# Expert 1's rows transposed by DMA instead of TensorE, and expert 0's second pass run with two weight pairs kept

## The chip, the cores and the metric

The program runs on one core of a Trainium2 chip. Its time is the device time of one execution in microseconds; a few executions are timed and the median is given. One further execution is recorded by the hardware profiler. The engines are TensorE (PE in the rows), its weight loads (PEld), VectorE (DVE), ScalarE (ACT), GpSimd (POOL) and SyncE (SP), which issues most transfers.

## The reference

Three stages, each on the output of the one before: block-causal attention, a mixture of 8 experts of which each token takes 2, and a dense layer pair.

```python
def _attn_ref(q, k, v):                       # q, k, v: 4 x 8 x 576 x 64
    scores = np.matmul(q, k.transpose(0, 1, 3, 2)) / np.sqrt(D)
    scores = np.where(mask, scores, -1e9)     # block of 64 rows sees its own and earlier blocks
    return softmax(scores) @ v                # rows of 8 heads joined: x is 2304 x 512
def _moe_ref(x, w_gate, w_noise, noise, w1, w2):
    noisy = x @ w_gate + np.log1p(np.exp(x @ w_noise)) * noise
    # the two largest of 8 per token, weights by softmax of the two
    out[mask] += weight * (np.maximum(x[mask] @ w1[e], 0) @ w2[e])   # 512 -> 1024 -> 512
def _moe2_ref(x, w_in, w_out):                # 512 -> 2048 -> 512
    h = x @ w_in
    return (h * np.clip(h + 3, 0, 6) / 6) @ w_out
```

## The kernel before

Precision is kept by splitting: each float32 operand becomes a rounded high part and the remainder as a low part, and each product is three matmuls, high by high, high by low, low by high (lines 464 to 466 for the first layer of an expert, 1178 to 1180 for the second). The high part of weights is a cast on ScalarE (line 415, `split_hi`), the low part a subtraction (line 419, `split_lo`), on VectorE here. Weights come in pairs of 128-column blocks, four pairs to an expert; `load_raw` (lines 380 and 382) issues two transfers a pair, on ScalarE's queue in the first ten steps of the expert loop.

Attention runs over 16 pairs of heads. It is ordered by a planner (class `Plan`): operations with durations, dependencies and priorities (a smaller number is more urgent) are put in an order by a list schedule, and the order is what is written out for each engine; on the chip the engines wait on semaphores only. A second planner run, `plan2`, orders what lies between attention and the expert loop: the routing of the last batch (`route`), the ranks of the experts by size (`ranks`), the row numbers of all experts (`slot_rows`), and the first pass of expert 0. Expert 0's tokens are known for three of four batches by then, so its first 256 rows (two tiles of 128) go through all eight 128-column blocks during routing. The priorities are in the table `PR`. As soon as the row numbers are there, three gathers on GpSimd (`load_x`, line 1147) fetch expert 0's other three tiles into buffers of the tag `xn`, of which there are five; each is transposed on TensorE (`x_tr`, line 432: four 128x128 transposes into an accumulation bank), rounded on ScalarE (`x_hi`, line 435) and subtracted on VectorE (`x_lo`, line 440). At the end of `plan2` the weight pair 0 is split again for the second pass.

Then comes the expert loop, written out by hand: steps `g`, one 128-column block of one expert each. Steps 0 to 7 are the second pass of expert 0 (columns 256 to 623 of its rows, tiles 2 to 4); steps 8 to 15 are expert 1 (544 rows in two halves of columns, 0 to 271 and 272 to 543), and so on. A step issues in this order: a split of the weight pair after the present one (`split`), at an expert's first step the gathers of the next expert's five tiles, the first layer (`e_s1`), loads of weights, the second layer of the step before (`e_s2`), and work on the next expert's rows. `s1` takes an accumulation bank of two for its output, with a third one (tag `x`) where `third` is set.

For the rows of the next expert there are two ways. Below `FIRST_TURNED` (2, so for expert 1) `x_tile` in steps 2 to 6 transposes one tile a step on TensorE, as above. From `FIRST_TURNED` on, `e_in` (line 1125) parts the 16-bit halves of the float32 row on ScalarE into a `pl` buffer (three of them) and SyncE issues a transposing DMA back into the `xn` buffer (line 1126); two or more steps later `e_out` joins the halves on ScalarE (line 1133) and rounds and subtracts as above, from the joined copy. The table `TURN_X` gives for each of the eight steps which tiles are joined and which are parted: parted are 0 and 1 in step 1, 2 in step 2, 3 in step 4, 4 in step 5; joined are 0 in step 3, 1 in step 4, 2 in step 5, 3 and 4 in step 6.

After the experts the rows are gathered again by token, weighted, and go through the dense layer pair; its weights arrive as 64-bit floats and are converted during the expert loop from step 8 on.

Of the kernel before, what the change touches and what calls it, by code (L numbers as in the profile page):

```python
# [7 lines left out]
F32 = mybir.dt.float32  # L8
# [17 lines left out]
AHEAD = 2  # L26
# [6 lines left out]
XB = 5  # L33
SLACK = 0.58
PLANES = ("w64", "ca", "w64", "cm")
TURNED = 2
FIRST_TURNED = 2
TURN_X = (((), ()), ((), (0, 1)), ((), (2,)), ((0,), ()), ((1,), (3,)), ((2,), (4,)), ((3, 4), ()), ((), ()))
CONV = (8, 5)
STICK = 2.77  # L40
# [3 lines left out]
PRE = ((0, 0), (1, 0))  # L44
WLS = ({"DVE": 1.2}, {"DVE": 1.14, "POOL": 2.4}, {"POOL": 2.4, "DVE": 1.14}, {"POOL": 2.4})
VHS = ({"POOL": 2.3}, {"DVE": 0.42}, {"POOL": 2.3, "DVE": 0.42}, {"DVE": 0.42, "POOL": 2.3}, {"ACT": 0.65, "DVE": 0.42})
PR = {'last': -400, 'ranks': 30, 'rows': -20.0, 'hold': 0.2, 'na': -563.0, 'nb': 803.0, 'lsel': (0, 0, 1, 0, 0, 0, 0, 0, 0, 0), 'f1': (-44.4, -71.8, 11.1, 5.5, -74.0, -35.6, -184.8, -17.0), 'f2': (-11.9, -48.6, 26.7, -35.2, 51.6, 79.6, -22.3, -2.7), 'fa': (-27.7, 2.3, 6.9, -8.3), 'fb': (-0.5, 4.2, -119.4, 2.2), 'fh': (12.0, -77.5, -123.7, -2.4, -13.0, -59.6, 12.4, 13.5), 'fl': (1.5, 3.1, -75.2, 108.2, -1.2, 70.3, 3.8, 16.9), 'v': -317.22, 'qk': -13.33, 'keep': 1, 'S': -2.19, 'max': -82.24, 'exp': -40.31, 'pt': 0.29, 'hi': 360.75, 'lo': -37.22, 'hid': True, 'av': 7.35, 'o': 252.33, 'od': True, 'inv': 36.95, 'fin': 28.78, 'x': -1.53, 'route': -0.9, 'rp': 1, 'route2': 6.36, 'xt': -802.7, 'eg': 587.2, 'ex': 432.13, 'ew': 2149.25, 'first': 0, 'sel': 2, 'vh': 3, 'wl': 1, 'wa': -418.9, 'wb': 581.9, 'h': -328.4, 's2': -471.5, 'vs': (-0.62, -2.53, 0.92, 0.17, 0.59, -5.66), 'vpt': (28.74, 8.73, -37.77, -2.51, -5.17, 6.9, -0.23, 1.96), 'vp': (-2.81, -6.08), 'vf': (15.46, 3.5)}
CLAMP = 122879.9921875


# [7 lines left out]
class Plan:  # L58
# [11 lines left out]
    def add(self, eng, fn, deps=(), prio=0.0, take=None, drop=None, lat=None, after=0.0, port=False, kind=None):  # L70

        if drop is not None:
            drop.left += 1
        self.ops.append((eng, fn, {d for d in deps if d is not None}, prio, take, drop, lat, port, kind))
        self.ready.append(after)
        return len(self.ops) - 1
# [110 lines left out]
def kernel(  # L187
# [216 lines left out]
    GR = [[(c, 0) for c in (1, 2)], [(c, 0) for c in range(3, NC)] + [(0, b) for b in range(0, B, 2)]]  # L404
    GR += [[(c, b) for c in range(1, NC)] for b in range(1, B)]
    PS = list(range(NPF)) + [st[0] * NPF + st[1] // 2 for st in STEPS[::2]]
    U0 = len(PS)
    PS += [NP + p for _ in GR for p in range(NFF // 2)]
    w_s = {}
# [728 lines left out]
    def turned_tile(key, t, n, to):  # L1138
# [3 lines left out]
        x_hi(to, t, x)  # L1142
        x_lo(to, t, x)

    def load_x(e, t):
        a = work.tile([128, DM], F32, tag="xn", name="xn", bufs=XB)
        nc.gpsimd.indirect_dma_start(
            out=a, out_offset=None, in_=x_tok[:, :],
            in_offset=bass.IndirectOffsetOnAxis(ap=(slot_ids if e else ids)[:, e * NT + t:e * NT + t + 1], axis=0),
        )  # L1150
        xn[e, t] = a
# [13 lines left out]
    def s2(tiles, h, wb, f, first, last, rows=None):  # L1165
        hh, hl = h
        wh, wl = wb
        for t in tiles:
            if first:
                yps[t] = ps_y.tile([128, DM], F32, tag=f"y{t}", name=f"y{t}")  # L1170
            n = min(128, (rows or CAP) - t * 128)
            if rows and t == NT - 1 and n <= 64:
                sl = slice(t * 128, t * 128 + 2 * n)
                nc.tensor.matmul(yps[t][:2 * n], lhsT=hh[:, sl], rhs=wh[:, f % 2], start=first, stop=False)
                nc.tensor.matmul(yps[t][:2 * n], lhsT=hh[:, sl], rhs=wl[:, f % 2], start=False, stop=last)
                continue
            sl = slice(t * 128, t * 128 + n)
            nc.tensor.matmul(yps[t][:n], lhsT=hh[:, sl], rhs=wh[:, f % 2], start=first, stop=False)  # L1178
            nc.tensor.matmul(yps[t][:n], lhsT=hh[:, sl], rhs=wl[:, f % 2], start=False, stop=False)  # L1179
            nc.tensor.matmul(yps[t][:n], lhsT=hl[:, sl], rhs=wh[:, f % 2], start=False, stop=last)  # L1180
# [227 lines left out]
    for f in range(NF + 1):  # L1408
        pr = 10 + 2 * f
        if f < NF and f % 2 == 0:  # L1410
            k2["wa", f // 2] = wops(0, f // 2, [k2.get(("s1", f - 4 + i)) for i in range(2)], pr + PR["wa"] + PR["fa"][f // 2])
        if f < NF and f % 2 == 0:
            k2["wb", f // 2] = wops(1, f // 2, [k2.get(("s2", f - 4 + i)) for i in range(2)], pr + PR["wb"] + PR["fb"][f // 2])
        if PR['first'] <= f < NF:
            g = Bank("h", 1)

            def first(e, f=f, g=g):
                ps = ps_y.tile([128, 512], F32, tag=f"y{NT - 1}", name="h") if g.bank == 2 else None
                g.tile = s1("a", f, f // 2, 0, n_, ps=ps)

            def second(e, f=f, g=g):
                hT["a", f] = h_tiles()
                h_hi(hT["a", f], g.tile, 0, n_)

            k2["s1", f] = add({"PE": 1.31}, first, [k2.get(("wa", f // 2))], pr + PR["f1"][f], take=g)
            hh = add({"ACT": 0.27}, second, [k2["s1", f], k2.get(("s2", f - HB))], pr + PR["h"] + PR["fh"][f], drop=g)
            k2["h", f] = add({"DVE": 0.34}, lambda e, f=f, g=g: h_lo(hT["a", f], g.tile, 0, n_), [hh], pr + PR["h"] + PR["fl"][f], drop=g)
        if f:
            k2["s2", f - 1] = add({"PE": 1.3}, lambda e, f=f - 1: s2(range(AHEAD), hT.pop(("a", f)), w_s[1, f // 2], f,
                                                                     f == 0, f == NF - 1),  # L1430
                                  [k2.get(("h", f - 1)), k2.get(("wb", (f - 1) // 2)), k2.get(("s2", f - 2))], pr + PR["s2"] + PR["f2"][f - 1])
    counts = work.tile([128, 16], F32, tag="counts", name="counts", bufs=1)[:, 0:E]
# [34 lines left out]
    c_ = add({"DVE": 1.75}, lambda e: ranks(psum(gn)), [c_], PR["ranks"], drop=gn, port=True)  # L1467
    add({"DVE": 1.4}, lambda e: slot_rows(), [c_, dp["id"]], PR["rows"], port=True)
    for t in range(AHEAD, NT):
        k2["g", t] = add({"POOL": 1.25}, lambda e, t=t: load_x(0, t), [dp["id"]], -10 + t, lat=3.0)  # L1470
        xops(t, k2["g", t], PR["xt"] + t)
    wops(0, NPF, [k2["s1", NF - 4], k2["s1", NF - 3]], PR["na"])
    wops(1, NPF, [k2["s2", NF - 4], k2["s2", NF - 3]], PR["nb"])
    plan2.run(busy, PR['last'] + 20, PR['hold'])
    gctx.close()
    wraw2[0] = ctx.enter_context(tc.tile_pool(name="wraw2", bufs=4, side="right", reuse_waits="tile"))
# [1 line left out]
    rr = route_rows()  # L1478
    NG = len(STEPS)
    conv = conv_ops()  # L1480
    last_use = {r: u for u, r in enumerate(PS)}
    load_at = {}
    for r in range(NPF, len(raw_q)):
        load_at.setdefault(max(2 * (last_use[r - 8] - NPF) if r >= 8 else 0, r - NPF), []).append(r)
    for g in range(NG + 1):
        u = NPF + g // 2 + 1
        if g < NG:
            e, f, _, _ = STEPS[g]
            if g % 2 == 0:
                split(0, u)  # L1490
            if f == 0 and e + 1 < E:
                for t in range(NT):
                    load_x(e + 1, t)
            if wide and g == CONV[0] - 1:
                conv_load(0)
            if g % 2 == 1:
                split(1, u)
            e_s1(g, FIRST_TURNED <= e + 1 and g < NG - NF)
            for r in load_at.get(g, ()):
                load_raw(r + 1, nc.scalar if g < 10 else None)  # L1500
        if g > NF and g % 3 == 0 and g // 3 - NF // 3 <= OVF // 4:
            zero_rows(g // 3 - NF // 3 - 1)
        if g == NF:
            nc.gpsimd.memset(zero, 0.0)
            for i in range(E):
                n = CAP - CAPS[i]
                nc.sync.dma_start(y_tab[i * CAP + CAPS[i]:(i + 1) * CAP].rearrange("p (k n) -> p k n", k=KD),
                                  zero[0:n, None, :].to_broadcast([n, KD, 128]))
        if wide and g >= CONV[0]:
            for _ in range(CONV[1]):  # L1510
                next(conv, None)
        if g == NG:
            overflow()
        if g:
            e_s2(g - 1)
        if g == NG - NF:
            for t in range(len(GR[0])):
                gather(0, t)
        for _ in range(2):
            if next(rr, None) == 0:  # L1520
                overflow_count()
        if g < NG and f >= 2 and f - 2 < NT and e + 1 < min(E, FIRST_TURNED):
            x_tile(e + 1, xn.pop((e + 1, f - 2)), f - 2, CAP)
        if g < NG and FIRST_TURNED <= e + 1 < E:
            outs, ins = TURN_X[f]
            for t in outs:
                e_out(e + 1, t)
            for t in ins:
                e_in(e + 1, t)
        if NG - NF + 4 <= g < NG - NF + 4 + len(GR[0]):  # L1530
            combine(0, g - (NG - NF + 4))
        if NG - NF + 5 <= g < NG - NF + 5 + len(GR[0]):
            combined(0, g - (NG - NF + 5))
# [93 lines left out]
```

## Time and profile before

| | us |
|---|---|
| median of 3 timed runs | 1066.28 (1065.69 to 1066.46) |
| profiled execution, whole | 1065.57 |
| profiled execution, span | 1063.8 |
| TensorE busy / VectorE / ScalarE / GpSimd, of the span | 1049.2 / 776.3 / 593.8 / 317.3 |

The mean granted TensorE clock is 0.998. The span is the time from the first to the last recorded instruction of the profiled execution. In the rows, a line of a timeline gives the start, the busy time, the engine (a `q` behind its name is its instruction queue), the line, the operation, output and inputs, the count, and in brackets how long the engine was idle before and what ended that. Durations of matmuls are modelled to the end of a pipeline, so that one starts before the one ahead of it has ended.

### The profile page before, as it was taken

Reading aid. Unit: us, or ns where it says so; the run is one execution under the profiler, and the core shown is the slowest. Engines: PE = TensorE matmul, PEld = TensorE weight load, DVE = VectorE, ACT = ScalarE, POOL = GpSimd, SP = SyncE. Lnnn points to the kernel's source line nnn. Section 1 sums busy time; section 2 is a strip of 40 time slices with the busy share of each in tenths; the row PEclk is TensorE's granted clock in tenths of the full one; section 3 lists DMA queues with packets and bytes.
Section 4 is the critical chain, followed back from the end, with each engine's and each line's share of the span. In section 5 each row is a group of like instructions: output and inputs, shape, how many; then the busy total and the mean of one; then the engine's idle time right before and its main releaser. Section 6 shows DMA issues by size and latency. Waiting matters only on the chain. (4 is left out here: it accounts for less than half of the span.)

```text
span 1063.8 us, 16944 instructions
## 1 busy us (share of the span) xinstructions
PE 1049.2 (99%) x6075; PEld 921.5 (87%) x6075; DVE 776.3 (73%) x1470; ACT 593.8 (56%) x1121; POOL 317.3 (30%) x379
## 2 busy tenths in 40 slices
PE   7999999999999999999999999999999999999998
PEld 6999999988988999999888898988888888888886
DVE  8878787878588998988787856775746755664442
ACT  6777777754456555655555445564535444454442
POOL 7558787713101120202020002733501511310000
PEclk9999999999999999999999999999999999999999
DMA  7534532114999999898887525212202211201001
GB/s 193 147 91 130 130 91 58 22 45 138 339 280 334 298 296 298 266 230 246 205 246 206 165 72 197 70 60 60 60 1 70 51 40 50 59 10 40 1 1 40
DMA packets 163573, 141.80 MB, mean 133 GB/s; under 512 B 92373, under 2 KB 131381, under 8 KB 163485
## 3 DMA queue, kind: packets, MB, share of 16 engines
q1 hardware_dynamic: 147501, 102.79, 35.2%
q0 software_dynamic: 8640, 28.32, 8.8%
q10 hardware_dynamic: 7344, 9.57, 2.7%
q8 instruction: 49, 0.80, 0.3%
q14 instruction: 39, 0.32, 0.1%
HBM read 92.94 MB, written 36.70 MB: 122 GB/s over the span
## 5 line engine op out<-in xcount | busy, mean ns | idle before, releaser
L464 PE MATMUL h<-xh,wah 128*128 128x512 f32 (+8 forms) x832 | 272.5, 328 | 0.7 <-ACT xh L435 0.7
L465 PE MATMUL h<-xl,wah 128*128 128x512 f32 (+8 forms) x832 | 271.2, 326 | 0.9 <-DVE xl L440 0.9
L466 PE MATMUL h<-xh,wal 128*128 128x512 f32 (+8 forms) x832 | 271.3, 326 | 0.0
L1179 PE MATMUL y<-wbl,hh 128*128 128x512 f32 (+1 forms) x576 | 225.7, 392 | 0.2
L1178 PE MATMUL y<-wbh,hh 128*128 128x512 f32 (+1 forms) x576 | 225.7, 392 | 0.1
L1180 PE MATMUL y<-wbh,hl 128*128 128x512 f32 (+1 forms) x576 | 225.0, 391 | 0.0
L464 PEld LDWEIGHTS h<-xh,wah 128*128 128x128 f32 x832 | 156.3, 188 | 16.2 <-ACT xh L435 1.1
L465 PEld LDWEIGHTS h<-xl,wah 128*128 128x128 f32 x832 | 156.4, 188 | 15.9 <-DVE xl L440 1.3
L466 PEld LDWEIGHTS h<-xh,wal 128*128 128x128 f32 x832 | 156.3, 188 | 11.5
L1180 PEld LDWEIGHTS y<-wbh,hl 128*128 128x128 f32 (+1 forms) x576 | 107.3, 186 | 24.8
L1179 PEld LDWEIGHTS y<-wbl,hh 128*128 128x128 f32 (+1 forms) x576 | 107.3, 186 | 21.5 <-POOL wbl L419 0.8
L487 ACT ACTIVATE hh<-h 128x288 fp32r<-128x288 f32 (+7 forms) x128 | 53.2, 417 | 130.2 <-PE h L466 129.7
L1178 PEld LDWEIGHTS y<-wbh,hh 128*128 128x128 f32 (+1 forms) x576 | 107.3, 186 | 21.2 <-issue 0.6
L1541 DVE SCALAR_TENSOR_TENSOR r<-r,h 128x512 f32<-128x512 f32 (+1 forms) x80 | 50.5, 631 | 98.2 <-ACT r L1540 98.0
L1540 ACT ACTIVATE r<-h,three 128x512 f32<-128x512 f32 (+1 forms) x80 | 51.6, 645 | 118.7 <-PE h L466 118.7
L419 DVE TENSOR_TENSOR wal<-wa,wah 128x1024 fp32r<-128x1024 f32 x80 | 106.3, 1328 | 11.2 <-ACT wah L415 10.2
L419 DVE TENSOR_TENSOR wbl<-wb,wbh 128x1024 fp32r<-128x1024 f32 x76 | 102.5, 1348 | 15.1 <-ACT wbh L415 14.9
L415 ACT CAST wbh<-wb 128x1024 fp32r<-128x1024 f32 x80 | 83.8, 1048 | 24.8 <-PE y L1180 14.6
L1543 ACT CAST hh<-r 128x512 fp32r<-128x512 f32 (+1 forms) x80 | 46.2, 577 | 86.0 <-DVE r L1541 86.0
L1544 DVE TENSOR_TENSOR hl<-r,hh 128x512 fp32r<-128x512 f32 (+1 forms) x80 | 56.0, 700 | 51.5 <-ACT hh L1543 51.5
L804 ACT ACTIVATE P<-sb,nm 128x192 f32<-128x192 f32 (+4 forms) x144 | 74.7, 528 | 29.1 <-DVE nm L798 29.0
L415 ACT CAST wah<-wa 128x1024 fp32r<-128x1024 f32 x80 | 83.7, 1046 | 2.4 <-DVE rm L1249 1.5
(275 smaller groups left out, 1780.9 us busy)
## 6 DMA issues: line engine op xcount, KB each, us to landing
wa<-in_moe_w_dram SPq DMA_DIRECT2D x23, 512.0 KB, 5.1
wb<-in_moe_w_dram SPq DMA_DIRECT2D x23, 512.0 KB, 5.6
y_tab<-yo SPq DMA_DIRECT2D x32, 256.0 KB, 4.3
w<-in_moe_w_in_dram SPq DMA_DIRECT2D x16, 512.0 KB, 5.3
y_tab<-zero SPq DMA_DIRECT2D x8, 1024.0 KB, 8.5
w<-in_moe_w_out_dram SPq DMA_DIRECT2D x16, 512.0 KB, 5.5
x_tok<-x SPq DMA_DIRECT2D x32, 144.0 KB, 2.8
wa<-in_moe_w_dram ACTq DMA_DIRECT2D x9, 512.0 KB, 6.6
```

The lines of the kernel that those rows point to most:

```text
L415: nc.scalar.copy(w_s[which, u][0], raws[PS[u]][which])
L419: (nc.gpsimd if e == "POOL" else nc.vector).tensor_tensor(lo, raws[PS[u]][which], hi.bitcast(F32), op=OP.subtract)
L464: nc.tensor.matmul(ps, lhsT=wh, rhs=xh, start=first, stop=False)
L465: nc.tensor.matmul(ps, lhsT=wh, rhs=xl, start=False, stop=False)
L466: nc.tensor.matmul(ps, lhsT=wl, rhs=xh, start=False, stop=last)
L487: nc.scalar.activation(h[0][:, c0:c1], ps[:, :c1 - c0], AF.Relu)
L804: nc.scalar.activation(o, views.pop((p, i)), AF.Exp, bias=nms.pop((p, i)), scale=1.0, accum_out=rs[p % 3][:, i:i + 1])
L1178: nc.tensor.matmul(yps[t][:n], lhsT=hh[:, sl], rhs=wh[:, f % 2], start=first, stop=False)
L1179: nc.tensor.matmul(yps[t][:n], lhsT=hh[:, sl], rhs=wl[:, f % 2], start=False, stop=False)
L1180: nc.tensor.matmul(yps[t][:n], lhsT=hl[:, sl], rhs=wh[:, f % 2], start=False, stop=last)
L1540: nc.scalar.activation(r[:, :n], ps[:, :n], AF.Relu, bias=three, scale=1.0)
L1544: nc.vector.tensor_tensor(hl[:, :n], r[:, :n], hh[:, :n].bitcast(F32), op=OP.subtract)
```

## The change

The rows of expert 1 take the second way too (`FIRST_TURNED` is 1): parted, transposed by DMA, joined, during steps 1 to 6; with it the first layer of expert 0's second pass uses the third accumulation bank. The second pass of expert 0 takes the weight pairs in the order 2, 3, 0, 1; pairs 2 and 3 are the last ones split in the first pass, and their splits are used again, so that pair 2 and 3 are not split a second time (`KEPT`); the two splits at the end of `plan2` and the two of steps 0 and 1 are gone. The three `xn` buffers of expert 0's late tiles are taken and touched early by a one-column write on GpSimd (`make_x`). The priorities of `plan2` are others, and the planner's durations for the two layers of the first pass are 1.345 and 1.385 instead of 1.31 and 1.3. By the new order the load of the tenth weight pair moves from step 5 to step 6.

```diff
-FIRST_TURNED = 2
+FIRST_TURNED = 1
-PR = {'last': -400, 'ranks': 30, 'rows': -20.0, 'hold': 0.2, 'na': -563.0, 'nb': 803.0, 'lsel': (0, 0, 1, 0, 0, 0, 0, 0, 0, 0), ... 'xt': -802.7, ... 'wa': -418.9, 'wb': 581.9, 'h': -328.4, 's2': -471.5, ...
+PR = {'last': -1000, 'ranks': 30, 'rows': 20.0, 'hold': 0.1, 'lsel': (0, 0, 0, 0, 0, 0, 0, 0, 0, 0), ... 'xt': -870.4, ... 'wa': -775.6, 'wb': 1670.1, 'h': -862.4, 's2': -314.7, ...
...
     PS = list(range(NPF)) + [st[0] * NPF + st[1] // 2 for st in STEPS[::2]]
+    KEPT = {NPF: NPF - 2, NPF + 1: NPF - 1}
+    PS[NPF:2 * NPF] = list(KEPT.values()) + list(range(NPF - 2))
...
+    def make_x(t):
+        xn[0, t] = work.tile([128, DM], F32, tag="xn", name="xn", bufs=XB)
+        nc.gpsimd.memset(xn[0, t][:, 0:1], 0.0)
+
     def load_x(e, t):
-        a = work.tile([128, DM], F32, tag="xn", name="xn", bufs=XB)
+        a = xn[e, t] if (e, t) in xn else work.tile([128, DM], F32, tag="xn", name="xn", bufs=XB)
...
-            k2["s1", f] = add({"PE": 1.31}, first, [k2.get(("wa", f // 2))], pr + PR["f1"][f], take=g)
+            k2["s1", f] = add({"PE": 1.345}, first, [k2.get(("wa", f // 2))], pr + PR["f1"][f], take=g)
...
     for t in range(AHEAD, NT):
-        k2["g", t] = add({"POOL": 1.25}, lambda e, t=t: load_x(0, t), [dp["id"]], -10 + t, lat=3.0)
+        made = add({"POOL": 0.1}, lambda e, t=t: make_x(t), [], -2000 + t)
+        k2["g", t] = add({"POOL": 1.35}, lambda e, t=t: load_x(0, t), [dp["id"], made], -10 + t, lat=3.2)
         xops(t, k2["g", t], PR["xt"] + t)
-    wops(0, NPF, [k2["s1", NF - 4], k2["s1", NF - 3]], PR["na"])
-    wops(1, NPF, [k2["s2", NF - 4], k2["s2", NF - 3]], PR["nb"])
     plan2.run(busy, PR['last'] + 20, PR['hold'])
...
-    last_use = {r: u for u, r in enumerate(PS)}
+    last_use = {r: u for u, r in enumerate(PS) if u not in KEPT}
+    for which in range(2):
+        for u, v in KEPT.items():
+            w_s[which, u] = w_s[which, v]
...
-            if g % 2 == 0:
+            if g % 2 == 0 and u not in KEPT:
                 split(0, u)
...
-            if g % 2 == 1:
+            if g % 2 == 1 and u not in KEPT:
                 split(1, u)
             e_s1(g, FIRST_TURNED <= e + 1 and g < NG - NF)
```

## Rows read from the trace of the kernel before

**Rows 1.** The page's first part: busy time, share of the span, instructions.
```profile
PE 1049.2 (99%) x6075; PEld 921.5 (87%) x6075; DVE 776.3 (73%) x1470; ACT 593.8 (56%) x1121; POOL 317.3 (30%) x379
```
**Rows 2.** TensorE's waits in the span: us in total, times, longest us.
```profile
...
PE h L465 <- DVE xl L440: 0.9, 2, 0.6
PE h L464 <- ACT xh L435: 0.7, 1, 0.7
PE xps L432 <- DVE idt L1456: 0.5, 1, 0.5
...
```
**Rows 3.** Timeline of TensorE, 251 to 257 us.
```profile
254.66 0.63 PE L432 MATMUL xps<-ident,xn 128*128 128x128 f32 x4 [0.48 <-DVE idt L1456]
...
256.69 0.44 PE L465 MATMUL h<-xl,wah 128*128 128x368 f32 x1 [0.29 <-DVE xl L440]
```
**Rows 4.** Timeline of TensorE, steps 1, 2, 3 and 8 of the expert loop.
```profile
262.71 0.33 PE L464 MATMUL h<-xh,wah 128*128 128x368 f32 x1
...
266.78 0.60 PE L432 MATMUL xps<-ident,xn 128*128 128x128 f32 x4
...
271.28 0.60 PE L432 MATMUL xps<-ident,xn 128*128 128x128 f32 x4
...
289.31 0.29 PE L464 MATMUL h<-xh,wah 128*128 128x272 f32 x1
...
290.83 0.28 PE L464 MATMUL h<-xh,wah 128*128 128x272 f32 x1
```
**Rows 5.** Timelines of VectorE and GpSimd: row numbers, first and third gather.
```profile
246.48 0.20 DVE L637 SCALAR_TENSOR_TENSOR ids<-idacc 128x40 int32<-128x40 f32 x1
...
247.51 1.44 POOL L1147 DMA_INDIRECT xn<-x_tok,ids  x1 [5.40 <-ACT hh L487]
...
251.12 0.95 POOL L1147 DMA_INDIRECT xn<-x_tok,ids  x1 [0.30 <-issue]
```
**Rows 6.** Engines' busy time and VectorE's costliest group, 229 to 256.6 us.
```profile
229.00:256.60 27.60, 25.64 (x174) 22.33 (x174) 25.23 (x90) 14.16 (x24) 5.58 (x5) 1.00 0.19 50
...
L419 DVE TENSOR_TENSOR wal<-wa,wah 128x1024 fp32r<-128x1024 f32 x4 | 4.9, 1218 | 0.5 <-ACT wah L415 0.4
```
**Rows 7.** ScalarE: groups of 305 to 339 us; timeline of step 1.
```profile
L1133 ACT COPY pl<-xn 128x1024 uint16<-128x1024 uint16 x5 | 6.8, 1366 | 2.5 <-DMA xn<-pl 2.5
...
L415 ACT CAST wah<-wa 128x1024 fp32r<-128x1024 f32 x3 | 3.1, 1049 | 0.0
...
L1125 ACT COPY pl<-xn 128x1024 uint16<-128x1024 uint16 x3 | 3.1, 1039 | 0.0
L435 ACT CAST xh<-pl 128x512 fp32r<-128x512 f32 x5 | 3.1, 622 | 0.2
...
264.89 0.48 ACT L487 ACTIVATE hh<-h 128x368 fp32r<-128x368 f32 x1 [0.58 <-PE h L466]
...
265.60 0.38 ACTq L382 DMA_DIRECT2D wb<-in_moe_w_dram  x1
```
**Rows 8.** Transposing DMAs: all 30; one issued in 325.4-327; one in 426-429.
```profile
DMA to landing us min/median/max: 3.1/6.6/9.9
...
xn<-pl SPq DMA_TRANSPOSE x1, 5.0
...
xn<-pl SPq DMA_TRANSPOSE x1, 3.1
```
**Rows 9.** Timelines, expert 1 to 2: last tile parted, joined; TensorE starts.
```profile
324.55 1.04 ACT L1125 COPY pl<-xn 128x1024 uint16<-128x1024 uint16 x1
...
332.51 1.37 ACT L1133 COPY pl<-xn 128x1024 uint16<-128x1024 uint16 x1
...
337.71 0.29 PE L464 MATMUL h<-xh,wah 128*128 128x288 f32 x1
```
**Rows 10.** Timelines of VectorE and TensorE near 7 us: parts of one tile.
```profile
6.50 1.15 DVE L773 SCALAR_TENSOR_TENSOR kl<-raw_k,kh 128x320 fp32r<-128x320 f32 x1
...
6.95 0.28 PE L790 MATMUL sb<-kl,qd0h 128*128 128x256 f32 x1
```

## What the change will do to the time

> **What bounds the kernel now.** I read the page's busy line first: TensorE (PE) is busy 99% of the span [rows 1]. Then all of PE's waits, grouped by what ended them: only three entries concern the experts, 2.1 us together, and all lie between 229 and 257 us [rows 2]; the others belong to attention, which the change leaves as it is. So a change can gain in two ways only: fewer PE instructions, or a shorter wait in that stretch. Then the PE timeline. In the second pass of expert 0 (steps 0 to 7 of the loop) the period is plain: step 1 runs from 262.71 to 266.78, 4.07 us; step 2, which carries four transposes of expert 1's rows, from 266.78 to 271.28, 4.50 us [rows 4]. Five steps carry them.
>
> The wait before the second pass lies at its three late row tiles: PE stands until the transposes of tile 4 at 254.66 (0.48 idle), again for its high part (0.7), again for its low part until 256.69 (one of the two in the 0.9) [rows 2, 3]. Behind tile 4 is the third gather: the row numbers are computed at 246.48, the first gather is issued at 247.51, the third at 251.12 [rows 5], and 3.5 us later PE transposes its rows.
>
> **The change part by part.** The sum is made against the profiled execution (1065.57 us, span 1063.8); the median of the three timed runs is 0.7 above it, and I add that at the end.
>
> *Expert 1's transposes leave PE.* 20 transposes in five steps: 5 x (4.50 - 4.07) = 2.2 us less PE work, all on the path, since PE waits for nothing in those steps [rows 2, 4]. This is certain as far as the rows go.
>
> *ScalarE does more.* Per tile it copies the halves apart (1.04), joins them (1.37) and rounds the result from SBUF (0.62, in place of a like rounding from PSUM) [rows 7]: 5 x 2.4 = 12 us more in eight steps of 4.07 us. Four casts of 1.05 are gone with the kept pairs [rows 7], two of them in these steps. The copies are hidden only as long as the last tile is ready when expert 1 begins. I follow ScalarE from the start of step 0, calling that 0. The activation of step g can start at 4.07 g + 2.2 (step 1: PE starts at 262.71, the activation is at 264.89 [rows 4, 7]). Step 4: activation at 18.5, two weight loads issued behind it until about 19.6 (the second issue starts 0.7 after the activation and is 0.4 long [rows 7]), tile 1 joined and rounded 2.0, tile 3 parted 1.0: 22.6. Step 5: cast 1.0, activation 0.5, tile 2 joined 2.0, tile 4 parted 1.0: 27.1. Then the transposing DMA, L us from issue to landing; then join and round 2.0, and VectorE's low part with its hand-over 0.9: ready at 30.0 + L. The first matmuls of expert 1 cover columns 0 to 271, so tiles 0 to 2; the second half starts 1.52 later [rows 4]. That the first half need not wait for the last tile is shown early in the span: a matmul at 6.95 reads part of a tile whose other part VectorE writes from 6.50 to 7.65 [rows 10]. So tile 4 is wanted at 8 x 4.07 + 1.5 = 34.1, and PE stands for L - 4.0. It stands at least 0.5, because step 6 issues two pairs of loads (four issues, some 2.2 us, from about 27.5) ahead of the joins of tiles 3 and 4 on ScalarE's queue: 29.7 + 4.0 + 0.9 = 34.6.
>
> For experts 2 and later the same chain has room: tile 4 parted at 324.55, joined at 332.51, PE starts the next expert at 337.71 [rows 9], because their steps work on five row tiles; expert 0's second pass has three, and that is the weak place of this change.
>
> L is not in the trace for this stretch. The ends are 3.1 and 9.9 us, the median 6.6; 3.1 belongs to a stretch in which nearly nothing else moved; 5.0 is a pair's first in a loaded stretch [rows 8]. I take 5.0: SP's queue carries nothing else in steps 1 to 6, and in steps 4 and 5 only one pair of weights is loaded, but two pairs come right behind the transpose. Stall 1.0; bounds 0.5 and 5.9.
>
> The rows show a transpose of the same 256 KB at three times its least time once other DMAs run [rows 8]. The Trainium skill, "DMA: Bandwidth & Descriptors", section "Latency and other measured facts", gives a DMA transpose 261 GB/s, and its section "Anatomy of one DMA" a fixed part of 2.0 us; an estimate from the two is 3.0 us, which agrees with the lowest row and would make the stall 0.5 and the time 1063.2. Its section "Issuing engines are not separate DMA queues" (all transfers interleave on the same 16 engines) speaks against counting on that here.
>
> *Kept pairs.* The order 2, 3, 0, 1 removes four casts on ScalarE and four subtractions on VectorE, of 1.22 each [rows 6]. Neither is on PE's path by itself. Two subtractions of them lay in the first pass, where VectorE is busy 25.2 of 27.6 us [rows 6], so demand falls to about 22.8. Loads: pair 1 of the third expert in turn is loaded one step later; it is used some ten steps on, so nothing.
>
> *Planner order, early buffers.* The last batch's routing gets a priority above all else, and the row buffers are touched on GpSimd (POOL) in advance. The first gather starts 0.83 after the row numbers end (246.68 to 247.51); behind the later list, whose buffers were free, it is a few tenths [rows 5], so about 0.55 is saved there. The rest depends on how much earlier the row numbers come. On VectorE's queue splits and low parts stand between the links of the routing chain; putting less than one split (1.22) behind it gives 0.9. Together 1.4. The upper bound is the whole wait: 1.45 of shown idle (0.48, 0.68, 0.29) plus some 0.2 for each, because modelled ends of matmuls overlap the next start: 2.1. The lower bound is below nothing: each split put behind routing comes later for PE in the first pass, up to a split and a low part, 1.6.
>
> *The rest.* The third accumulation bank for this pass costs nothing and removes no wait. The first wait, at the start of the first pass (the other in the 0.9 [rows 2]), comes from attention's end and stays. ScalarE is the engine behind whose loads the joins queue in step 6; SP's queue gets five transposes ahead of the conversion's first load, which then goes out after them, and is not used before step 8.
>
> Sum: 2.2 + 1.4 - 1.0 = 2.6 us less: 1063.0 for a profiled execution, 1063.7 as a median.
>
> **Rivals.**
> 1. Nothing is late: transposes land in 3.1, routing wins all. 2.2 + 2.1 - 0.5 = 3.8: 1062.5. For it: ScalarE's copies may overlap more tightly than I add them. Against: two pairs of loads in step 6.
> 2. The last tile is late by the median row: L = 6.6, stall 2.6, net 1.0: 1065.3. For it: nearly all transposes under load lie at 5 or above [rows 8].
> 3. Routing first starves PE in the first pass: the wait moves from the late tiles to the splits, gain there 0, net 1.2: 1065.1. For it: VectorE has little free time there [rows 6]; against: 2.4 us of its work are gone.
> 4. Slower: the same place as rival 2, with the longest row. From L = 7.6 the stall (3.6) eats all that the rest brings; at 9.9 it is 5.9, net loss 2.3: 1068.6. Against: 9.9 is one of 30, and SP's queue is emptier here.
> That the change doesn't do what it says is excluded for the transposes (they are gone from the code); for the routing it is rival 3.
>
> **How the numbers follow.** Forecast 0.45, rival 1 0.17, rival 2 0.20, rival 3 0.11, rival 4 0.07. What a measurement can tell from no change is about 0.2%, 2.1 us. The forecast's own spread (L of 4.5 to 5.5, routing 0.9 to 1.9) is about 0.8 either way, so 0.32 of its 0.45 lies beyond 2.1, with rival 1 0.49 faster; 0.44 the same; 0.07 slower. The range runs from just beyond rival 1, 1062.2, past rivals 2 and 3 to 1067.0, where L is 8.3.
>
> **What would show it.** Period of steps 2 to 6 of the second pass 4.07 us, no transposes on PE. Second pass starting 1.4 earlier than 256.7, with the row numbers about 0.9 earlier and a first gather a few tenths behind them. A wait of about 1 us on PE about 1.5 us into expert 1, ended by the low part of its last tile, and ScalarE idle there for the transposing DMA. I am wrong if that wait is above 2 us or missing, if PE waits inside the first pass for a split, or if expert 1 waits at its first matmul.

## The result, and the profile after

| | before | after |
|---|---|---|
| median of 5 timed executions, us | 1066.18 (1065.69 to 1066.46) | 1081.66 (1078.63 to 1083.68) |
| profiled execution, whole / span, us | 1065.57 / 1063.8 | 1083.68 / 1081.9 |

The ratio is 1.014, with a 95% interval of 1.0128 to 1.0151: the changed kernel is 15.5 us slower, where 2.6 us less were forecast; the time lies 14.7 us above the upper end of the range. The new one also scatters by 5 us from execution to execution, the old one by 0.8. Between the profiled executions, of which that of the changed kernel is the slowest of its five, the difference is 18.1 us, and that is the one I account for.

TensorE's busy time (first part of the page) is 4.3 us up on [rows 1], though 20 transposes are gone from it:

```profile
PE 1053.5 (97%) x6055; PEld 923.2 (85%) x6055; DVE 771.8 (71%) x1467; ACT 600.3 (55%) x1127; POOL 315.2 (29%) x381
```

What PE waited for, in the view of [rows 2] (us in total, times, longest us); line numbers are two higher than before as far as `e_out`, now line 1135, and six higher from `load_x`, now line 1153, to the second layer:

```profile
PE y L1184 <- ACT hh L489: 8.0, 2, 7.0
PE h L466 <- ACT xh L437: 5.5, 1, 5.5
...
PE h L467 <- DVE xl L442: 0.9, 2, 0.6
PE h L466 <- issue: 0.7, 1, 0.7
...
PE y L1186 <- DVE hl L493: 0.6, 1, 0.6
```

The 0.9 and the 0.7 are those of [rows 2]. The rest is new: 14.2 us. The timeline of PE shows where:

```profile
282.09 0.50 PE L1184 MATMUL y<-wbh,hh 128*128 128x512 f32 x1 [1.04 <-ACT hh L489]
...
283.43 0.50 PE L1186 MATMUL y<-wbh,hl 128*128 128x512 f32 x1 [0.61 <-DVE hl L493]
...
294.38 0.80 PE L1184 MATMUL y<-wbh,hh 128*128 128x512 f32 x1 [6.98 <-ACT hh L489]
...
305.99 0.59 PE L466 MATMUL h<-xh,wah 128*128 128x272 f32 x1 [5.54 <-ACT xh L437]
```

The last line is the second half of step 8, the first matmul that reads the last tile of expert 1. The long wait before it, for the activation `hh` of step 6, is no wait for rows. ScalarE's timeline says what stood ahead of that activation:

```profile
262.19 1.99 ACT L1127 COPY pl<-xn 128x1024 uint16<-128x1024 uint16 x2 [0.72 <-issue]
...
266.73 1.05 ACT L1127 COPY pl<-xn 128x1024 uint16<-128x1024 uint16 x1 [1.21 <-issue]
...
271.92 1.35 ACT L1135 COPY pl<-xn 128x1024 uint16<-128x1024 uint16 x1 [2.52 <-DMA xn<-pl]
...
277.76 1.35 ACT L1135 COPY pl<-xn 128x1024 uint16<-128x1024 uint16 x1 [2.51 <-DMA xn<-pl]
...
281.56 0.47 ACT L489 ACTIVATE hh<-h 128x368 fp32r<-128x368 f32 x1
290.08 1.33 ACT L1135 COPY pl<-xn 128x1024 uint16<-128x1024 uint16 x1 [8.05 <-DMA xn<-pl]
...
291.97 1.04 ACT L1127 COPY pl<-xn 128x1024 uint16<-128x1024 uint16 x1
...
293.86 0.47 ACT L489 ACTIVATE hh<-h 128x368 fp32r<-128x368 f32 x1
...
303.96 1.33 ACT L1135 COPY pl<-xn 128x1024 uint16<-128x1024 uint16 x1 [7.75 <-DMA xn<-pl]
```

Line 1127 parts a tile, line 1135 joins one. Tile 2 is parted by 267.78 and can be joined at 290.08: 22.3 us for the transposing DMA and its issue. ScalarE stands idle for 8.05 us of that, with tile 4's parting (291.97) and the activation of step 6 (293.86) behind the join in its queue. Tile 4 is thus parted only by 293.01, 37.0 us after step 0 began; where no loads ran beside the transposes (an experiment below) it was 25.2 us. Its own DMA then takes 10.95, from 293.01 to 303.96. The first two tiles, parted by 263.2 and 264.2, were joined at 271.92 and 277.76.

Granted clock (columns of the view of [rows 6]; the number after the engines is the clock as a share of full speed, then DMA share, GB/s):

```profile
290.00:292.00 2.00, 0.00 (x0) 0.00 (x0) 0.00 (x0) 1.88 (x3) 0.32 (x1) 0.95 1.13 247
292.00:294.00 2.00, 0.00 (x0) 0.00 (x0) 0.70 (x2) 2.00 (x4) 0.63 (x1) 0.50 0.94 211
294.00:296.00 2.00, 1.50 (x3) 0.78 (x4) 1.97 (x4) 1.97 (x3) 0.17 (x1) 0.50 1.03 372
296.00:298.00 2.00, 2.00 (x5) 1.49 (x6) 0.78 (x2) 0.21 (x1) 0.78 (x1) 0.50 1.05 352
298.00:300.00 2.00, 2.00 (x13) 1.81 (x12) 0.00 (x0) 0.00 (x0) 0.00 (x0) 0.84 1.10 336
...
306.00:308.00 2.00, 1.87 (x6) 1.56 (x7) 1.74 (x2) 2.00 (x3) 0.72 (x2) 0.50 0.69 208
308.00:310.00 2.00, 2.00 (x9) 1.90 (x9) 1.97 (x6) 0.88 (x3) 0.00 (x0) 0.50 0.90 202
310.00:312.00 2.00, 2.00 (x7) 1.49 (x6) 1.93 (x7) 0.01 (x1) 0.00 (x0) 0.50 1.01 342
312.00:314.00 2.00, 2.00 (x14) 1.81 (x13) 1.93 (x4) 0.00 (x0) 0.00 (x0) 0.93 1.12 339
```

While PE stood before 294.38 the clock fell to its lower level, 1.2 GHz, and stayed there for some 4 us of work; the same after the second stand, for some 6. Summed over these stretches, PE's busy time times the share of the clock that was missing is 5.1 us.

The account: step 0 starts at 255.97 (before: 255.96), step 9 at 312.79 (before: 294.36), 18.4 us later. New waits 14.2, half clock 5.1, transposes gone -2.2 (five times 0.43): 17.1. Of the other 1.3 us half is in the modelled ends of matmuls: from the start of one matmul to the start of the next the four stands cost 0.16 more each than their idle time (the last is 5.83, less the 0.13 by which its neighbours follow each other, against 5.54). The rest I did not find in single rows. After step 9 the difference changes by only 0.3, from 18.4 to 18.1.

### The profile page after: what moved, and what is told of

It reads as the page before. It is cut to its first block, busy times and chain, and to the rows that moved or that the text cites. A ratio compares the mean times of both kernels' runs of the same rounds, so it can differ in the third digit from the quotient of the medians.

```text
span 1081.9 us, 16914 instructions
## 1 busy us (share of the span) xinstructions
PE 1053.5 (97%) x6055; PEld 923.2 (85%) x6055; DVE 771.8 (71%) x1467; ACT 600.3 (55%) x1127; POOL 315.2 (29%) x381
## 5 line engine op out<-in xcount | busy, mean ns | idle before, releaser
L1185 PEld LDWEIGHTS y<-wbl,hh 128*128 128x128 f32 (+1 forms) x576 | 108.2, 188 | 20.8
L421 DVE TENSOR_TENSOR wal<-wa,wah 128x1024 fp32r<-128x1024 f32 x78 | 103.8, 1331 | 12.9 <-ACT wah L417 11.5
L421 DVE TENSOR_TENSOR wbl<-wb,wbh 128x1024 fp32r<-128x1024 f32 x74 | 100.0, 1352 | 16.2 <-ACT wbh L417 14.3
L493 DVE SCALAR_TENSOR_TENSOR hl<-h,hh 128x288 fp32r<-128x288 f32 (+8 forms) x128 | 56.2, 446 | 41.4 <-ACT hh L489 37.3
```

What stands on the lines that cost most here:

```text
L421: (nc.gpsimd if e == "POOL" else nc.vector).tensor_tensor(lo, raws[PS[u]][which], hi.bitcast(F32), op=OP.subtract)
L493: nc.vector.scalar_tensor_tensor(h[1][:, c0:m], ps[:, :m - c0], 0.0, h[0][:, c0:m].bitcast(F32), op0=OP.max, op1=OP.subtract)
```

## Experiments

Three theories of why the rows of expert 1 come late. **Theory 1:** the transposing DMAs, alone on SP's queue, get a small share of the engines while the weight loads come from ScalarE's queue. **Theory 2:** the stretch has too many bytes to move, from whichever queue. **Theory 3:** ScalarE's 12 us of copies do not fit, and the DMA's time does not matter. Ratios are to the kernel before on the same chip, with 95% intervals.

**The change without the new way for expert 1.**

```diff
-FIRST_TURNED = 1
+FIRST_TURNED = 2
```

> The changed kernel with FIRST_TURNED back at 2: expert 1's rows are transposed by PE again; the pair order 2, 3, 0, 1, the kept pairs, the early row buffers and the new planner orders stay. All three theories below put the loss on the transposing DMAs and give 1065.5 to 1066.5 us here: the second pass of the changed kernel began at 256.70 us as before, so I now count the kept pairs at nothing, where the prediction counted -1.4. If kept pairs or orders cost something by themselves, it is over 1067.

Measured 1066.93 us, ratio 1.0006 (0.9997 to 1.0015): no difference that can be told. So kept pairs, early buffers and new orders do not make the loss, nor do the orders and buffers bring the 1.4 us forecast for them (the prediction had the 1.4 there, and not at the kept pairs, as the expectation says). From the end of PE's wait at the start of the first pass to step 0 it is 25.8 us here, 26.0 before.

**The new way alone, in the kernel before.**

```diff
-FIRST_TURNED = 2
+FIRST_TURNED = 1
```

> The kernel before with FIRST_TURNED at 1 and nothing else: the transposing DMAs for expert 1 without kept pairs. If the transposing DMAs alone make the loss, about 1078 to 1084 us, with waits of 5 to 7 us of PE for expert 1's rows. If it needs the kept pairs' order too (which moves the loads of steps 4 to 7), under 1070.

Measured 1077.74 us, ratio 1.0127 (1.0099 to 1.0156), 0.3 under the range of the first theory. The new way alone makes nearly the whole loss, by the same two kinds of wait; PE's timeline of this run:

```profile
280.21 0.50 PE L1178 MATMUL y<-wbh,hh 128*128 128x512 f32 x1 [2.58 <-ACT hh L487]
...
297.93 0.47 PE L464 MATMUL h<-xh,wah 128*128 128x272 f32 x1 [2.97 <-ACT xh L435]
```

The waits are shorter than the 5 to 7 us expected, in an execution of 1074.54 us, the fastest of the four; in it the first two transposes were the slow ones, joined 12 and 16 us after their parting, and the last took 7.

**Without the five transposing DMAs.**

```diff
-        nc.sync.dma_start_transpose(...)
+        if e != 1:
+            nc.sync.dma_start_transpose(...)
...
+        how = "p (n w) -> p w n" if e == 1 else "p (w n) -> p w n"
```

> The changed kernel without the five transposing DMAs of expert 1; ScalarE makes the same copies, and expert 1 computes on rows that were not transposed (that part of the output is left wrong). Theories 1 and 2 (the DMA's landing is what is late): 1062 to 1064.5 us, with PE waits for expert 1's rows of under 1 us, which would also be the forecast's rival 1. Theory 3 (ScalarE's 12 us of copies are too much for these steps, or stand in the wrong place): over 1070 us, hh still late.

Measured 1065.12 us, ratio 0.9989 (0.9979 to 0.9998). All of ScalarE's copies are there (the join reads its rows in another order here, in the same 1.36 us), and PE waits for no row of expert 1. Theory 3 falls. Against the run with PE's transposes on the same chip (1066.93) it is 1.8 us less: that is what the transposes are worth on the path, 2.2 forecast. The time is 0.6 above the 1062 to 1064.5 expected; those numbers still held the 1.4 us that the run before last doesn't show.

**Loads on SP's queue.**

```diff
-                load_raw(r + 1, nc.scalar if g < 10 else None)
+                load_raw(r + 1)
```

> The changed kernel with one word changed: the weight loads of the first ten steps are issued by SP, as those of the later steps are, not by ScalarE. Theory 1 (the transposing DMA's packets get a small share while loads come from ScalarE's queue): each transposing DMA lands 4 to 9 us after its issue, PE's waits shrink to under 2 us, 1063 to 1068 us. Theory 2 (too many bytes in these steps, whatever the queue): landings stay at 9 to 21 us, 1078 to 1084 us. Theory 3 (ScalarE's in-order copies hold h_hi up, the DMA's time does not matter): 1078 to 1084 us.

Measured 1070.99 us, ratio 1.0036 (1.0024 to 1.0048): over two thirds of the loss is gone with the same bytes and the same copies, for one word. It is theory 1's direction, though not down to its 1068. From the views of PE's waits and of the transposing DMAs (256 to 292 us):

```profile
PE h L466 <- ACT xh L437: 2.3, 1, 2.3
```

```profile
DMA to landing us min/median/max: 5.6/7.7/9.9
```

In the changed kernel the same view has 12.6/12.8/12.9 for those it could pair, without the one of over 20 us.

**A plain copy of the same bytes in the transpose's place.**

```diff
+        if e == 1:
+            nc.sync.dma_start(src.bitcast(U16), pl)
+        else:
             nc.sync.dma_start_transpose(...)
```

> The changed kernel, its loads from ScalarE's queue as they are, but for expert 1 the transposing DMA is a plain copy of the same 256 KB from the one tile to the other (2,048 bytes of a row at a time, so expert 1's rows are not transposed and that part of the output is left wrong). If the small packets of the transpose (256 bytes each) are what gets a small share beside the loads: landings of 3 to 6 us, waits of PE under 1.5 us, 1064.5 to 1067 us. If any DMA on SP's queue gets half the share or less while ScalarE's queue loads: landings of 8 us and more, 1072 us or more.

Measured 1067.76 us, ratio 1.0014 (1.0005 to 1.0024): 0.8 over the upper end of the one theory and far below the 1072 of the other. Loads on ScalarE's queue beside a plain copy on SP's do little harm. All transfers from 264 to 276 us, first of the changed kernel, then of this run (q1 is SP's queue, q10 ScalarE's, q0 GpSimd's; packets, MB, share of 16 engines):

```profile
DMA packets 3909, 2.84 MB, mean 237 GB/s; under 512 B 2197, under 2 KB 3367, under 8 KB 3909
...
q10 hardware_dynamic: 1783, 2.31, 71.3%
q1 hardware_dynamic: 2126, 0.53, 45.0%
```

```profile
DMA packets 2898, 4.09 MB, mean 341 GB/s; under 512 B 152, under 2 KB 1697, under 8 KB 2897
...
q10 hardware_dynamic: 2448, 3.22, 83.1%
q1 hardware_dynamic: 432, 0.79, 17.5%
q0 software_dynamic: 17, 0.07, 1.5%
```

With the transposes the packets' time adds up to more (116% of the engines against 102%), and 30% fewer bytes are moved; even the loads alone, 2.31 MB against 3.22. ScalarE waits for such a DMA 20.8 us in all in the one, 1.4 in the other (view of ScalarE's waits, changed kernel from 256.6 to 310 us, then this run to 292):

```profile
ACT pl L1135 <- DMA xn<-pl: 20.8, 4, 8.1
```

```profile
ACT pl L1138 <- DMA xn<-pl: 1.4, 2, 0.9
```

So it is not the second queue as such, nor the bytes: it is the transposing DMA together with loads from another queue. Whether its small packets do it or the transposing itself was not separated, since a plain copy differs in both. And the fewer bytes moved are not the other queue's doing alone: from 264 to 276 us the run with the loads on SP's queue moved 220 GB/s, and one with them behind the transposes (below) 285. What that queue shortens is the wait for a transpose.

**The loads moved out of steps 1 to 6.**

```diff
+        at = max(2 * (last_use[r - 8] - NPF) if r >= 8 else 0, r - NPF)
-        load_at.setdefault(max(...), []).append(r)
+        load_at.setdefault(0 if r < 6 else max(at, 7 + (r - 6) // 2), []).append(r)
```

> The changed kernel with the loads of steps 1 to 6 moved: one pair more at step 0, the others from step 7 on; still from ScalarE's queue. Tiles 2, 3 and 4 are then transposed with no loads beside them. If the loads beside them make the landings late (from whichever queue), tiles 2 to 4 land in 3 to 5 us, PE waits under 1 us for rows, and the time is 1064.5 to 1066.5 us unless the loads that now crowd steps 7 to 12 come late, which would show as waits of PE for weights. If the transposing DMAs are slow by themselves when several of them run, 1068 us or more.

Measured 1078.80 us, ratio 1.0110 (1.0088 to 1.0133). On the landing it came out as expected: ScalarE parts tile 4 until 282.46 and joins it at 286.41, so 3.9 us, and PE waits for no row. The price is paid elsewhere: the issues of the loads moved to step 7 stand in ScalarE's queue ahead of its next cast, VectorE waits for that cast, and PE for VectorE (timelines of ScalarE, its queue, VectorE and PE):

```profile
281.42 1.04 ACT L1127 COPY pl<-xn 128x1024 uint16<-128x1024 uint16 x1
...
286.41 1.36 ACT L1135 COPY pl<-xn 128x1024 uint16<-128x1024 uint16 x1 [0.70 <-DMA xn<-pl]
...
295.39 0.38 ACTq L380 DMA_DIRECT2D wa<-in_moe_w_dram  x1
...
296.64 1.05 ACT L417 CAST wah<-wa 128x1024 fp32r<-128x1024 f32 x1 [6.90 <-DMA y_tab<-zero]
...
297.72 1.23 DVE L421 TENSOR_TENSOR wal<-wa,wah 128x1024 fp32r<-128x1024 f32 x1 [6.28 <-ACT wah L417]
...
299.35 0.59 PE L466 MATMUL h<-xh,wah 128*128 128x272 f32 x1 [4.30 <-DVE hl L493]
...
317.07 0.60 PE L466 MATMUL h<-xh,wah 128*128 128x272 f32 x1 [3.70 <-DVE hl L493]
```

Five pairs (5 MB) were put off, and the steps that got them have no room for them. It is not that weights come late, as the expectation feared: the pair cast at 296.64 had been loaded in step 0. What the issue at 295.39 waited for the rows don't show.

**Loads on SP's queue, behind the transposes of their step.**

```diff
-            for r in load_at.get(g, ()):
-                load_raw(r + 1, nc.scalar if g < 10 else None)
...
+        for r in load_at.get(g, ()):      # after e_out and e_in
+            load_raw(r + 1)
```

> The changed kernel with all loads from SP's queue, and in each step behind the transposing DMAs, not ahead of them. In the run with loads from SP ahead (1071.0 us), tile 3 took about 10 us and PE waited 2.3 us for the last rows. If what was left there is the queue's order (each transposing DMA stands behind 1 or 2 MB of loads), this run has landings of 4 to 7 us and 1065 to 1068 us. If the sum of bytes was what was left, it stays at 1070 to 1072 us.

Measured 1068.83 us, ratio 1.0036 (1.0025 to 1.0047): between the two ranges expected, and no different from the loads ahead, in total. In the trace it is another story. Tile 4 is parted until 280.60 and joined at 286.00 (5.4), PE waits for no row of expert 1, and step 9 starts 36.6 us after step 0 (before: 38.4): 1.8 us of gain are there. It is lost again later. Waits of ScalarE, VectorE and PE from 257 to 430 us:

```profile
ACT pl L1135 <- DMA xn<-pl: 18.4, 7, 5.9
DVE ca L1082 <- DMA w<-in_moe_w_in_dram: 9.6, 5, 4.5
...
PE y L1184 <- DVE yo L1197: 2.2, 3, 1.3
```

In the kernel before the first two are 2.8 and 2.6 in that stretch, and the last is missing. The rows of experts 2 and later and the conversion's loads now come late, and VectorE, which the conversion holds up, copies the results out of the accumulation banks too late for PE. At the end of the span this execution is 3.3 us behind the kernel before, counted from step 0, so 5.1 are lost after step 9; PE's waits for `yo` and `hl` there add up to 3.4, and the rest is not accounted for.

**Loads on SP's queue and moved out of steps 1 to 6.** The edits of two runs above together.

> Both: loads from SP's queue and those of steps 1 to 6 moved to step 0 and to steps 7 and later. Landings of 3 to 5 us for tiles 2 to 4, which is as good as they come: by the run without transposing DMAs (1065.1 us, 1.8 under the one with PE's transposes) 1065 to 1066.5 us, if no weights come late. If it is over 1068 us, something other than the landing holds expert 1's rows up.

Measured 1076.42 us, ratio 1.0093 (1.0076 to 1.0110). Tile 4 takes 3.9 us, as expected, and PE waits for no row of expert 1; but it waits 1.6 us at 308 and 6.6 us at 328 behind VectorE, the second time because VectorE waits for rows of expert 2. Their first transposing DMA is issued at 314.81 only, 17 us after the tile is parted, behind what is crowded in SP's queue (309.70 in the run above), and joined at 323.43. It was not something else that held expert 1's rows up, as my expectation had it for this case: the lateness went to the next expert (SP's queue, PE):

```profile
314.81 4.16 SPq L1128 DMA_TRANSPOSE xn<-pl  x2
...
328.02 0.59 PE L466 MATMUL h<-xh,wah 128*128 128x272 f32 x1 [6.62 <-DVE hl L493]
```

**The same place in the queue, without the transposing DMAs.** The edit of the third run on top of the loads on SP behind the transposes.

> The run with all loads on SP's queue behind the transposing DMAs (1068.8 us), without the five transposing DMAs; ScalarE's copies stay, and expert 1 computes on rows that were not transposed (that part of the output is left wrong). If what was left there is the transfers' own time on the 16 engines, which are busy without a break from 257 to 430 us, so that the conversion's loads and the weights come later: 1064.5 to 1066 us. If it is the loads' new place in SP's queue: 1068 us or more, as with them.

Measured 1065.39 us, ratio 0.9988 (0.9978 to 0.9998). So the place of the loads costs nothing, and the 4.3 us between this and the run with the DMAs (1.2 below and 3.1 above the kernel before) are the transfers' own. The two waits of ScalarE and VectorE shown above are 6.7 and 2.2 us here, and PE's is 0.7. To that extent theory 2 holds: beside small packets from another queue, the plain time of the transposes on engines that are never free here costs more than PE's transposes did while the conversion begins at step 8.

**The conversion two steps later**, with the loads on SP behind the transposes.

```diff
-CONV = (8, 5)
+CONV = (10, 5)
```

> The run with all loads on SP's queue behind the transposing DMAs, with the conversion of the shared expert's weights begun two steps later (step 10, not 8). In the run without this VectorE waited up to 4.5 us for a conversion's load, and PE 2.9 us for copies of the results behind it. If the conversion's loads are what the transposing DMAs push back: waits of PE for yo under 1 us and 1065 to 1067 us. If the transfers delay the weights whatever the conversion does: 1068 to 1070 us.

Measured 1067.09 us, ratio 1.0003 (0.9993 to 1.0013), PE's waits for `yo` 0.7: 0.1 above the upper end of the first theory, and as fast as the kernel before.

**The same in the kernel before, with the new way but no kept pairs.**

> The kernel before with FIRST_TURNED at 1, loads on SP's queue behind the transposing DMAs, and the conversion from step 10: everything but the kept pairs and the new orders. If the kept pairs are worth nothing, as the run with them alone had it, this is within 1 us of the run with them, 1064.5 to 1067 us. If the kept pairs' fewer copies of ScalarE and VectorE help once ScalarE has the rows too, it is 2 us or more above that run.

Measured 1069.71 us, ratio 1.0027 (1.0015 to 1.0038), 2.6 us above the run with kept pairs. PE's wait for expert 1's last rows, here and in the run above:

```profile
291.06 0.39 PE L464 MATMUL h<-xh,wah 128*128 128x272 f32 x1 [1.99 <-ACT xh L435]
```

```profile
289.78 0.39 PE L466 MATMUL h<-xh,wah 128*128 128x272 f32 x1 [0.32 <-ACT xh L437]
```

Whether that is the casts that the kept pairs save, the load that their order moves out of step 5, where tile 4 is transposed, or the new orders and early buffers, which differ too, was not separated.

**The conversion two steps later in the kernel before.**

> The kernel before with the conversion begun at step 10, and nothing else: what that is worth by itself. PE waits for nothing in the steps concerned in the kernel before, so by every theory 1066 to 1066.8 us; if it is under 1065.5 us, what the two runs with it gain is not the transposing DMAs'.

Measured 1066.85 us, ratio 1.0010 (0.9994 to 1.0026): nothing by itself, as expected. What it gained beside the transposing DMAs (from a ratio of 1.0036 to 1.0003) comes from their side. The second run with it has no partner without it.

No version that I tried beats the kernel before by more than a measurement can tell. The least that the idea could reach is given by the runs without the DMAs, 0.1% below before.

## Why the prediction was wrong

**What bounds the kernel** was read rightly: PE sets the end, and what was found of the loss is waits of PE and PE at the lower clock.

**The transposes' 2.2 us** were somewhat high: 1.8 between two runs on one chip. The 4.07 us were read from step 2, the only one of steps 2 to 7 in the kernel before whose first layer ran at 0.166 us a matmul; in the others it was 0.174, and four transposes move the next matmul by 0.35 (266.78 to 267.13), not 0.43. A step at that pace without them takes 4.15 (the run without the DMAs), and five times 0.35 is the 1.8.

**ScalarE's 12 us** were right, and hide even better than I had them: with no DMA to wait for, the minimum stall of 0.5 is not there.

**The step that failed is L**, the time of the transposing DMA, and its reason above all: "I take 5.0: SP's queue carries nothing else in steps 1 to 6". It was 8.7 for the first tile, some 11 for the last and over 20 for the third. The empty queue was no help: with the loads put on it too, a transpose took 5.6 to 9.9. The 30 transposes of [rows 8] nearly all run in steps whose loads go out on SP's queue too, and from step 10 on always; I took their spread as bounds for a stretch in which the loads come from ScalarE's queue, and 9.9 was no upper end there. [rows 7] show the loads on that queue, a line under the activation; I used them for ScalarE's time only. The Trainium skill's rule that I cited against it, "DMA: Bandwidth & Descriptors", section "Issuing engines are not separate DMA queues", points the right way in that a queue of one's own is no capacity of one's own. But by it the queue of the loads should not matter either, and moving them was worth some 11 us here. The estimate of 3.0 that I made from the same page of the Trainium skill used a fixed part which it gives for DMAs of GpSimd's path, where these are SP's: with no loads beside it the last tile took 3.9.

**The sum followed one tile only.** I put the stall at the last tile, L - 4.0. With L of 11 that is 7, and PE's wait there is 5.5. But each of the five DMAs has a join waiting for it in ScalarE's queue, ahead of an activation that PE needs: tile 2's held PE up for 6.98 late in the second pass, and with the waits of the first two joins it made tile 4's start some 12 us late. Nothing in my working asks what is queued behind a join. Rival 4 had the place and the sign, with L of 9.9 as its end and one wait instead of two.

**The lower clock** was not in the sum: 5.1 us, more than any of its terms.

**Kept pairs at nothing** holds for the change itself (1.0006). With rows that come nearly in time the run with them, the new orders and the buffers was 2.6 us faster than the one without, so something of these is worth more than I had it. The load that the order moves by a step, which I set at nothing because its weights are used late, may be part of that.

**Planner order, 1.4 us**, did not come. The row numbers and the first gather in the changed kernel (timelines of VectorE and GpSimd), against [rows 5]:

```profile
246.87 0.20 DVE L639 SCALAR_TENSOR_TENSOR ids<-idacc 128x40 int32<-128x40 f32 x1
...
247.81 1.57 POOL L1153 DMA_INDIRECT xn<-x_tok,ids  x1 [19.14 <-DVE hl L493]
```

Attention ended 0.24 later in this execution, so the row numbers came 0.15 later than before, not 0.9 sooner; and the gather starts 0.74 after them, not a few tenths: 0.09 saved of 0.55. So the busy buffers were not what delayed the first gather. Step 0's second matmul starts at 256.70, before at 256.69 [rows 3]. That is what rival 3 gave for this place, gain 0; PE waits inside the first pass for nothing, though, so its mechanism was another. Counted from the start of the first pass, some 0.2 are gained.

**A slip without effect:** what I called step 1 (262.71, [rows 4]) is step 2, since step 0 has no second layer and takes 2.7 us. Both ends of the chain move by one period, and L - 4.0 stays.

## What to carry to other kernels

Before a transfer of small packets is put on the path, look at what else is under way in that stretch, from which queue, and take its duration only from rows with the same neighbours; if there are none, the longest row is no upper bound. Where an engine runs in order, ask of every wait that is added what stands behind it, not only of the last one of a series. And where the DMA share is 1.0, as here, look for the place where transfers that are pushed back come due: a gain won at the start of the stretch can be given back there.

## What was unexpected in the hardware

Transposing DMAs and weight loads from another queue slow each other: 237 GB/s together against 341 with plain copies in the transposes' place, over the same 12 us, and in the changed kernel one transpose of 256 KB took over 20 us, against 3.9 with no loads beside it. With both on one queue a transpose took 5.6 to 9.9 us.

Part of that is there without any neighbour. In the kernel before, from 532.5 to 533.5 us, one transposing DMA has the engines to itself, and keeps them all busy at 208 GB/s:

```profile
DMA packets 813, 0.21 MB, mean 208 GB/s; under 512 B 813, under 2 KB 813, under 8 KB 813
...
q1 hardware_dynamic: 813, 0.21, 109.2%
```

From 264 to 276 us, where it moves loads and gathers with no transpose, it is 370 GB/s at a DMA share of 0.9 or more throughout. So a transpose takes the engines' time of nearly twice its bytes.

PE's clock went to 1.2 GHz while PE stood for 7.0 and 5.5 us, and was back at 2.4 only some 4 and 6 us after it had begun again. In the first run with the loads on SP's queue it stood at 0.50 from 290 to 296, after a wait of 2.3.

The matmuls of the first layer in the second pass followed each other by 0.166 us in some of the profiled executions (the changed kernel and the new way alone, until PE first waits) and from step 3 on by 0.173 to 0.175 in others (the kernel before, the run without the DMAs), which makes a step without transposes 4.05 or 4.15 us. What makes the difference stays open.
